# Attention and an expert layer on one core: float64 weights turned in fewer passes, seven-product matmuls for the first two batches too, and the order of every engine as a written list

## The chip, the cores and the metric

One core of a Trainium2 chip runs one program. Its engines are TensorE (PE, with its weight loads PEld), VectorE (DVE), ScalarE (ACT), GpSimd (POOL) and SyncE (SP, which here only issues DMAs). The metric is the device time of one execution in microseconds (us).

## What is computed

For each of 8 batches and 8 heads, 512 tokens of 64 numbers read from 32 state rows by a softmax, and the state rows read from the tokens by another. The results, 544 rows of 512 per batch, go through a normalisation and a two-layer network with a residual:

```python
a = softmax(scale * x @ state.T);   xread = a @ state
a2 = softmax(scale * state @ x.T);  sread = a2 @ x
x = concat([xread, sread])                      # 8 x 544 x 512
xn = (x - mu) / sqrt(var + 1e-06) * g_ln
out = x + max(xn @ w_ch1, 0) @ w_ch2            # 512 -> 2048 -> 512
```

x and state arrive as float32; g_ln as float32; the two weight matrices arrive as float64 and are read as pairs of 32-bit words.

## The kernel before, in words

Every matmul operand is held as a pair of float16 tiles (hi, and lo for what hi leaves out), and a product is three matmuls (`TERMS`). The network's hidden width of 2048 is cut into four units u of 512.

**A batch.** `attention(b)` loads x and the state, scales and splits x, transposes by DMA, makes scores (L214), both softmaxes, `sread` (L259, L269) and the tokens' reads (L300, evicted by ACT on L302). It ends in `normalise`, whose last steps cut the result into pairs `pc` (ACT makes hi, DVE makes lo) and transpose them by DMA into `xnT` (L343). Then come the **first products** (xnT times w_ch1) and the **second products** (hidden times w_ch2, L612), which `ffn` runs for batch b while it pulls `attention(b + 1)` forward a step at a time. After the last batch the sreads of all batches go through the same network as one batch of 256 rows.

**Two kinds of first product.** For batches 2 to 7 and for the state rows, `first_product` forms each 2 x 2 block product from seven half-size products (Strassen's scheme, L570): 336 matmuls of 256 columns per batch, with sums of blocks on DVE and POOL around them. It needs sums of weight blocks (`weight_sums`, made during batch 1) and of xn blocks (`pieces`). For batches 0 and 1 `first_product_plain` (L551) takes 192 matmuls of 512 columns, and `normalise` cuts its pairs without sums (L359).

**The weights.** `convert` turns each unit of either matrix in two halves of 128 x 1024. For a half, ACT takes the sign (L447) and the magnitude (L416) of the high words, DVE bounds it and takes its maximum (L417), shifts it (L418) and joins it with the low words (L419); then, with the unit's scale known, ACT scales (L453), POOL gives the sign back (L454), ACT makes hi (L461) and POOL lo (L462). `common_scale` brings the four units of w_ch2 to one scale when all are there, by multiplying the tiles in place on DVE (L540).

**Order.** The tile framework's scheduler orders each engine's instructions from the order of the code. For the head (batch 0, the attention of batch 1 and all weights) `PLAN` says how many steps of which generator come next; batch 0 goes through the second products unit by unit as weights become ready. Each engine runs its instructions in order, and so does the SP queue with the DMAs.

Of the kernel before, what the change touches and what calls it, by code (L numbers as in the profile page):

```python
# [20 lines left out]
F64_MIN = 2.0**-15  # L21
F64_AMAX = 2.0**-12
# [4 lines left out]
SW1 = 2.0**3  # L27
# [15 lines left out]
TERMS = ((0, 0), (0, 1), (1, 0))  # L43
COMPUTE = (mybir.EngineType.Activation, mybir.EngineType.DVE, mybir.EngineType.Pool)
# [3 lines left out]
def moe_attention(ctx: ExitStack, tc: tile.TileContext, x, state, g_ln, w1, w2, out):  # L48

# [41 lines left out]

    def accumulator():
        return ps_f.tile([P, 512], F32, name="acc")

    def banks():
        return ps_a.tile([P, 2, 512], F32, name="banks")

    def column(pool, name, n=1):
        return pool.tile([P, n], F32, name=name)


    def load_batch(b):
# [12 lines left out]
    loaded = {0: load_batch(0)}
# [20 lines left out]
    def across(a, name):


        n = a.shape[1]
        ps = ps_x.tile([P, 512], F32, name="spread")  # L140
        nc.tensor.transpose(ps[0:n, 0:P], a, idf)
        top = column(small, name + "_t")
        nc.vector.tensor_reduce(top[0:n], ps[0:n, 0:P], AX.X, ALU.max)
        nc.tensor.matmul(ps[:, P:P + n], lhsT=top[0:n].broadcast_to([n, P]), rhs=idf[0:n, 0:n], start=True, stop=True)
        return ps[:, P:P + n]

    def absmax(a, t):
# [15 lines left out]
    marks = {}  # L163
    sread_rows = tc.dram_tile([B * NS, DM], F32, name="sread_rows")

    def attention(b):
        if b not in loaded:
            loaded[b] = load_batch(b)
            yield
        xf, sj, sr = loaded.pop(b)  # L170
        xfl = xf.rearrange("p h c d -> p (h c) d")
        am, part = column(small, "x_am", 2), column(small, "x_part", 4)
        x16 = rows("x16").bitcast(F16).rearrange("p (a i d) -> p a i d", i=2, d=D)
        for q in range(4):
            v = slice(8 * q, 8 * q + 8)
            if q % 2 == 0:
                nc.scalar.activation(x16[:, v].bitcast(BF16)[:, :, 0], xfl[:, v], AF.Abs, accum_out=part[:, q:q + 1])
            else:
                absmax(part[:, q:q + 1], xfl[:, v].rearrange("p a d -> p (a d)"))
            yield  # L180
        absmax(am[:, 0:1], part)
        absmax(am[:, 1:2], sj.rearrange("p g d -> p (g d)"))
        m = column(small, "x_m", 2)
        nc.vector.tensor_scalar_max(m, across(am, "x"), TINY)
        sc, isc = scales(m, SX, "x")
        sx, sst, isx, isst = sc[:, 0:1], sc[:, 1:2], isc[:, 0:1], isc[:, 1:2]
# [547 lines left out]
```

## Time and profile before

| | us |
|---|---|
| median of 3 runs | 864.38 |
| lowest, highest | 862.9, 864.95 |
| the profiled execution, its own time | 863.29 |
| its span, first to last instruction | 861.5 |
| TensorE busy | 742.0 |
| VectorE busy | 543.6 |
| ScalarE busy | 331.3 |
| GpSimd busy | 215.0 |

The profiled execution took 1.8 us more than its span, and 1.1 less than the median. A row of a timeline gives start, duration, engine, line, operation, out<-in and shapes, how many instructions are merged in it, and in brackets the idle time of the engine before it and what ended that. VectorE's instructions overlap a little at their ends, so that one after another they advance by less than their durations.

### The profile page before, as it was taken

The numbers are of one execution on the slowest core, as the hardware profiler recorded it, in microseconds if no ns is written. First come the engines' busy times: TensorE is split into PE (matmuls) and PEld (weight loads), VectorE is DVE, ScalarE is ACT, GpSimd is POOL, SyncE is SP. The second block draws the span as 40 slices with busy tenths as digits, with TensorE's granted clock in tenths as the row PEclk, the third lists the DMA queues.
The fourth block names the chain that finished last, engine by engine and source line by source line (L and its number), as shares of the span: only waits on it lengthen the run. The fifth ranks groups of instructions, "written<-read, shape, count | busy, mean of one in ns | idle before, by whom it ended". The sixth has DMA issues, their size and how long they took to land.

```text
span 861.5 us, 12789 instructions
## 1 busy us (share of the span) xinstructions
PE 742.0 (86%) x5184; PEld 453.2 (53%) x5184; DVE 543.6 (63%) x897; ACT 331.3 (38%) x534; POOL 215.0 (25%) x137
## 2 busy tenths in 40 slices
PE   0230998964999899999989899989998999999997
PEld 0130443521434487548744685478546854784483
DVE  5999778788783568456836584648565856562050
ACT  4484765233541344134413452235234523341030
POOL 0076664175750202021112021202111211020010
PEclk9999999976999999999999999999999999999999
DMA  8952414513033551262333633443335232402000
GB/s 214 314 182 38 159 49 107 138 50 98 10 60 78 121 116 32 53 141 62 60 70 97 112 57 66 118 79 59 76 88 117 51 77 54 107 2 43 25 27 24
DMA packets 146586, 73.83 MB, mean 86 GB/s; under 512 B 125472, under 2 KB 137248, under 8 KB 146080
## 3 DMA queue, kind: packets, MB, share of 16 engines
q1 hardware_dynamic: 146384, 72.77, 35.5%
q8 instruction: 40, 0.66, 0.3%
q10 hardware_dynamic: 144, 0.26, 0.2%
q14 instruction: 18, 0.15, 0.1%
HBM read 28.57 MB, written 9.44 MB: 44 GB/s over the span
## 4 chain that ended last, share of the span: by engine, by line
PE 54%; DVE 20%; DMA 14%; issue 4%; ACT 3%; SPq 3%; POOL 2%; DVEq 0%; ACTq 0%
PE acc L570 24%; PE acc L612 23%; DMA xnT<-pc 5%; PE acc L551 4%; DMA raw<-in_moe_w_ch_dram 3%; DVE pc L383 2%; DVE w_t L419 2%; DMA s_r<-in_state_dram 2%; DVE pc L359 2%; DMA ebT<-eb 2%; DVE x L200 1%; DVE w_t L417 1%; DVE xm L348 1%; DMA x_f<-in_x_dram 1%; SPq L343 1%
## 5 line engine op out<-in xcount | busy, mean ns | idle before, releaser
L612 PE MATMUL acc<-w2h,hid 128*128 128x512 f16 x1632 | 364.4, 382 | 8.5 <-ACT w2h L461 4.1
L570 PE MATMUL acc<-xnT,w1c 128*128 128x256 f16 (+1 forms) x2352 | 250.2, 268 | 14.3 <-DMA xnT<-pc 13.2
L612 PEld LDWEIGHTS <-hid 128*128 128x128 f16 x1632 | 159.2, 99 | 196.3 <-issue 11.7
L570 PEld LDWEIGHTS <-w1c 128*128 128x128 f16 x2352 | 216.6, 99 | 48.1 <-issue 17.6
L551 PE MATMUL acc<-xnT,w1c 128*128 128x512 f16 x384 | 90.4, 391 | 16.8 <-DMA xnT<-pc 16.5
L596 POOL TENSOR_TENSOR m<-u,m 128x512 f32<-128x512 f32 (+1 forms) x28 | 33.4, 1194 | 234.1 <-DVE u L595 174.2
L551 PEld LDWEIGHTS <-w1c 128*128 128x128 f16 x384 | 37.8, 100 | 64.9 <-issue 24.7
L629 DVE SCALAR_TENSOR_TENSOR xr<-acc,uo,xr 128x512 f32<-128x512 f32 x28 | 21.0, 749 | 78.0 <-PE acc L612 78.0
L302 ACT ACTIVATE xr<-banks,ux 128x1024 f32<-128x1024 f32 x14 | 15.6, 1114 | 105.3 <-PE banks L300 103.9
L338 POOL TENSOR_TENSOR rs<-rs,mhalf 128x4 f32<-128x4 f32 (+1 forms) x9 | 12.3, 1367 | 169.7 <-DVE rs L337 120.7
L454 POOL TENSOR_TENSOR w_t<-w_t,sgn 128x1024 f32<-128x1024 f32 x16 | 36.4, 2300 | 62.3 <-ACT w_t L453 62.3
L578 ACT ACTIVATE hid<-u 128x512 f16<-128x512 f32 (+1 forms) x56 | 32.9, 593 | 26.5 <-DVE u L599 21.6
L333 DVE BATCH_NORM_STATS2 s<-xr 128x6 f32<-128x512 f32 x32 | 20.7, 684 | 33.7 <-ACT xr L302 33.7
L579 DVE SCALAR_TENSOR_TENSOR hid<-u,hid 128x512 f16<-128x512 f32 (+1 forms) x56 | 38.9, 707 | 2.1 <-ACT hid L578 2.1
L383 DVE TENSOR_TENSOR pc<-xn,pc 128x512 f16<-128x512 f32 (+1 forms) x28 | 23.7, 878 | 25.0 <-ACT pc L382 25.0
L579 DVE SCALAR_TENSOR_TENSOR hid<-acc,hid 128x512 f16<-128x512 f32 (+1 forms) x28 | 18.1, 645 | 33.3 <-ACT hid L578 33.3
L583 ACT ACTIVATE m<-acc 128x512 f32<-128x512 f32 (+1 forms) x28 | 15.6, 556 | 54.6 <-PE acc L570 40.9
L245 POOL TENSOR_TENSOR ts<-ts,mA 128x1024 f32<-128x1024 f32 x8 | 16.1, 2008 | 54.9 <-DVE mA L244 53.1
L589 ACT ACTIVATE m<-acc 128x512 f32<-128x512 f32 (+1 forms) x28 | 15.8, 566 | 33.7 <-PE acc L570 24.1
L348 DVE SCALAR_TENSOR_TENSOR xm<-xr,mv,gx 128x512 f32<-128x512 f32 x32 | 28.7, 917 | 0.0
L382 ACT ACTIVATE pc<-xn 128x512 f16<-128x512 f32 (+1 forms) x28 | 15.1, 588 | 32.5 <-DMA xnT<-pc 32.4
L554 ACT ACTIVATE hid<-acc 128x512 f16<-128x512 f32 x32 | 18.7, 592 | 22.7 <-PE acc L551 22.7
(128 smaller groups left out, 892.0 us busy)
## 6 DMA issues: line engine op xcount, KB each, us to landing
raw<-in_moe_w_ch_dram SPq DMA_DIRECT2D x16, 1024.0 KB, 6.1
x_f<-in_x_dram SPq DMA_DIRECT2D x16, 512.0 KB, 5.8
out_dram<-xr SPq DMA_DIRECT2D x16, 512.0 KB, 3.0
ek<-ea SPq DMA_DIRECT2D x56, 64.0 KB, 2.0
ek<-ek SPq DMA_DIRECT2D x7, 512.0 KB, 4.2
s_r<-in_state_dram SPq DMA_DIRECT2D x32, 64.0 KB, 5.0
s_j<-in_state_dram SPq DMA_DIRECT2D x8, 64.0 KB, 2.2
sread_rows<-sread SPq DMA_DIRECT2D x32, 16.0 KB, 3.3
```

The lines of the kernel that those rows point to most:

```text
L333: nc.vector.bn_stats(s6, xr[t][:, c])
L348: nc.vector.scalar_tensor_tensor(xm, xr[t][:, c], mv[:, n, 0:1], gx, ALU.subtract, ALU.mult)
L383: nc.vector.tensor_tensor(pc[:, q, 1], v, pc[:, q, 0], ALU.subtract)
L454: nc.gpsimd.tensor_tensor(t, t, sgn[:, fh], ALU.mult)
L551: nc.tensor.matmul(ps, lhsT=w1c[u][:, q // 2 * 2 + k // 2, i, k % 2, q % 2 * P:(q % 2 + 1) * P], rhs=xT[:, k // 2 * 2:k // 2 * 2 + 2, j, k ...
L554: nc.scalar.activation(hid[:, 0, q], ps, AF.Relu)
L570: nc.tensor.matmul(ps[:, f * w:(f + 1) * w], lhsT=w1c[u][:, A_PIECE[m], i, k, f * P:(f + 1) * P], rhs=xT[:, m, j, k * w:(k + 1) * w], star ...
L578: nc.scalar.activation(hi, v, AF.Relu)
L579: nc.vector.scalar_tensor_tensor(lo, v, 0.0, hi, ALU.max, ALU.subtract)
L596: nc.gpsimd.tensor_tensor(m5, u3, m5, ALU.add)
L612: nc.tensor.matmul(po, lhsT=hid[:, i, q, c * P:(c + 1) * P], rhs=w2h[u][:, j, q], start=first and q == 0 and n == 0, stop=last and q == 3 ...
L629: nc.vector.scalar_tensor_tensor(v, po, uo, v, ALU.mult, ALU.add)
```

## The change

**Conversion** (`load`, `split`). Per half, ACT multiplies the high words in place by 2^-112, POOL multiplies them by zero, which leaves a signed zero, DVE joins it with the shifted low words and then with the shifted high words, and ACT takes the sum of magnitudes for the scale. Then ACT makes hi and DVE lo, both with the scale in the instruction. The sums of blocks of w_ch1 are taken by POOL from the float32 values before the split, four per unit, and all seven blocks are split.

**Seven products for all batches.** `first_product_plain`, the plain branch of `normalise` and `weight_sums` are gone. Products are scaled as they leave PSUM, by `hs[u]` and `hn[u]`, so `common_scale` makes four small instructions and no pass over w_ch2. The first of the evicted blocks goes through ACT into a strip `r` before it is split.

**Order.** All functions yield closures, one for each step, and `issue` runs them in the order of the lists `PLAN`, `BATCH` (batches 1 to 6) and `LAST`, with the framework's scheduler off. Of these lists one line is shown.

```diff
-    def magnitudes(raw, t, most):
...
-        nc.scalar.activation(t, raw[:, :, 1].bitcast(F32), AF.Abs)
-        nc.vector.tensor_scalar(t, t, F64_MIN, F64_AMAX, ALU.max, ALU.max, accum_out=most)
-        nc.vector.tensor_scalar(ti, ti, 7 << 27, 3, ALU.bitwise_xor, ALU.logical_shift_left)
-        nc.vector.scalar_tensor_tensor(ti, low, 29, ti, ALU.logical_shift_right, ALU.bitwise_or)
...
-            nc.scalar.activation(t, t, AF.Abs, scale=s)
-            nc.gpsimd.tensor_tensor(t, t, sgn[:, fh], ALU.mult)
...
-            nc.scalar.activation(hi, t, AF.Copy)
-            engine.tensor_tensor(lo, t, hi, ALU.subtract)
...
+            yield do(nc.scalar.activation, high.bitcast(F32), high.bitcast(F32), AF.Copy, scale=REBIAS)
+            yield do(nc.gpsimd.tensor_tensor, t, high.bitcast(F32), zero.broadcast_to([P, 1024]), ALU.mult)
+            yield do(nc.vector.scalar_tensor_tensor, low, low, 29, t.bitcast(U32), ALU.logical_shift_right,
+                     ALU.bitwise_or)
+            yield do(nc.vector.scalar_tensor_tensor, t.bitcast(U32), high.bitcast(U32), 3, low, ALU.logical_shift_left,
+                     ALU.bitwise_or)
+            yield do(nc.scalar.activation, raws[fh].bitcast(BF16)[:, 0:1024], t, AF.Abs, accum_out=am[:, fh:fh + 1])
...
+    def split(hi, lo, t, s):
+        yield do(nc.scalar.activation, hi, t, AF.Copy, scale=s)
+        yield do(nc.vector.scalar_tensor_tensor, lo, t, s, hi, ALU.mult, ALU.subtract)
...
+        yield do(nc.gpsimd.tensor_tensor, s1, a21, a22, ALU.add)
...
-        for u in range(U):
-            v = w2h[u].rearrange("p i q e -> p (i q e)")
-            nc.vector.tensor_scalar(v, v, ratio[:, u:u + 1], None, ALU.mult)
...
+        do(nc.vector.tensor_scalar, hs, uoq, r, SH, ALU.mult, ALU.mult)()
+        nc.vector.tensor_scalar(hn, hs, -1.0, None, ALU.mult)
...
+        yield do(nc.scalar.activation, r, p1, AF.Relu, scale=sp)
+        yield from finish(r, 0, 0)
...
+    "a1 a0 c0 b1 a3 a2 c1 a4-5 b0 a6-12 a60 a13 a27 a19 a28 a17 a20 a14 a18 a24 a15 c2 a16 a25 a22 c3 k2 a23 "
...
+        with tc.manual_schedule():
...
+    issue([attention(0), *map(weights1, range(U)), first_products(0, h, True), *map(weights2, range(U)), attention(1),
+           second_products_by_units()], PLAN)
     common_scale()
...
+    for b in range(1, B - 1):
+        issue([first_products(b, h), second_products(b, h, store_batch), attention(b + 1)], BATCH)
+    issue([first_products(B - 1, h), second_products(B - 1, h, store_batch), state_rows(), first_products(B, 1),
+           second_products(B, 1, store_state)], LAST)
```

**What stands in a row.** Three places on VectorE. In the kernel after, most closures run from one line, so rows read L104 and tell by their tiles: `raw` the float64 words, `w_t` the float32 weights, `w1c` and `w2h` the split weights, `strips` the evicted blocks of a first product, `hid` the split hidden values, `xr` the residual rows, `acc` and `banks` PSUM tiles.

VectorE in the middle of the head, where a half of w_ch2 is turned beside batch 0's first products, before:

```order
L417 TENSOR_SCALAR w_t,w_am<-w_t 128x1024
L555 SCALAR_TENSOR_TENSOR hid<-acc,hid 128x512 x2
L418 TENSOR_SCALAR w_t<-w_t 128x1024
L419 SCALAR_TENSOR_TENSOR w_t<-raw,w_t 128x1024
L555 SCALAR_TENSOR_TENSOR hid<-acc,hid 128x512
L143 TENSOR_REDUCE w_t<-spread 2x1
```

and after:

```order
L104 SCALAR_TENSOR_TENSOR raw<-raw,w_t 128x1024
L104 SCALAR_TENSOR_TENSOR w1c<-sums,w_s,w1c 128x512
L104 SCALAR_TENSOR_TENSOR w_t<-raw 128x1024
L104 SCALAR_TENSOR_TENSOR strips<-acc,strips 128x512
L104 SCALAR_TENSOR_TENSOR w1c<-w_t,w_s,w1c 128x512
```

Between the steps of the conversion there stand now splits of w_ch1, which read two tiles of SBUF each; before there stood evictions, which read PSUM and one tile.

VectorE at the end of the head, where the last scale of w_ch2 is known and batch 1 is normalised, before:

```order
L533 TENSOR_REDUCE uo<-uoq 128x1
L348 SCALAR_TENSOR_TENSOR xm<-xr,mv,gx 128x512 x2
L536 RECIPROCAL r<-uo 128x1
L537 TENSOR_SCALAR ratio<-uoq,r 128x4
L540 TENSOR_SCALAR w2h<-w2h,ratio 128x4096 x3
```

and after:

```order
L104 TENSOR_REDUCE uo<-uoq 128x1
L104 SCALAR_TENSOR_TENSOR xn<-xr,mv,gx 128x2x256
L104 RECIPROCAL r<-uo 128x1
L104 SCALAR_TENSOR_TENSOR w2h<-w_t,w_s,w2h 128x1024
L104 TENSOR_SCALAR hs<-uoq,r 128x4
L104 SCALAR_TENSOR_TENSOR w2h<-w_t,w_s,w2h 128x1024
```

The three passes over a whole unit are gone, and the two lo halves of the last unit stand there, which GpSimd made before.

VectorE around the end of a middle batch, from the second pair of statistics (`rs`) to the last pair of the next batch's `pc`, before:

```order
L337 TENSOR_SCALAR rs<-mv 128x4
L348 SCALAR_TENSOR_TENSOR xm<-xr,mv,gx 128x512
L148 TENSOR_REDUCE x_part<-x_f 128x1
L376 TENSOR_TENSOR tq<-xn 128x512
L383 TENSOR_TENSOR pc<-xn,pc 128x512 x2
L376 TENSOR_TENSOR tq<-xn,tq 128x512
L148 TENSOR_REDUCE x_part<-x_f 128x1
L383 TENSOR_TENSOR pc<-tq,pc 128x512
L629 SCALAR_TENSOR_TENSOR xr<-acc,uo,xr 128x512
```

and after:

```order
L104 TENSOR_SCALAR rs<-mv 128x4
L104 SCALAR_TENSOR_TENSOR xr<-acc,uo,xr 128x512
L104 TENSOR_TENSOR tq<-xn 128x512
L104 TENSOR_TENSOR pc<-xn,pc 128x512
L104 TENSOR_TENSOR tq<-xn,tq 128x512
L104 TENSOR_TENSOR pc<-tq,pc 128x512 x2
L104 TENSOR_TENSOR pc<-xn,pc 128x512 x3
L104 SCALAR_TENSOR_TENSOR xr<-acc,uo,xr 128x512
```

One more eviction of a second product (`xr<-acc`) stands behind the statistics, and the reductions of the following batch's x no longer stand between the pieces.

## Rows read from the trace of the kernel before

**Rows 1.** The page's shares of the chain of work that ended last, by engine.
```profile
PE 54%; DVE 20%; DMA 14%; issue 4%; ACT 3%; SPq 3%; POOL 2%; DVEq 0%; ACTq 0%
```

**Rows 2.** Busy time by stretch: the stretch, its length, then for PE, PEld, DVE, ACT and POOL the busy time (and instructions), then the granted clock of TensorE, the DMA share and GB/s. The cuts are the starts of first products, and in the last three the starts of the last batch's first and second products and of the state rows.
```profile
7.50:85.55 78.05, 15.02 (x168) 11.15 (x168) 72.11 (x126) 47.31 (x62) 32.55 (x14) 1.00 0.66 187
85.55:206.70 121.15, 96.62 (x488) 43.38 (x488) 99.23 (x154) 59.28 (x79) 63.94 (x32) 0.91 0.35 96
...
478.32:563.05 84.73, 84.73 (x619) 55.68 (x619) 53.76 (x89) 33.05 (x58) 13.14 (x9) 0.98 0.42 85
...
652.55:737.48 84.93, 84.93 (x619) 55.72 (x619) 53.43 (x89) 33.33 (x56) 13.17 (x9) 0.98 0.33 72
737.48:775.75 38.27, 37.17 (x338) 32.88 (x337) 24.29 (x41) 14.82 (x27) 7.19 (x7) 1.00 0.17 41
775.75:817.19 41.44, 41.44 (x196) 18.84 (x194) 6.01 (x11) 2.81 (x6) 0.20 (x1) 1.00 0.15 35
817.19:861.50 44.31, 39.48 (x432) 27.91 (x429) 14.13 (x35) 8.48 (x24) 2.92 (x4) 1.00 0.08 25
```

**Rows 3.** Timeline of PE at the starts of batches (and the DMA issue ahead of batch 1's first product): start, us, what.
```profile
202.21 4.30 SPq L343 DMA_TRANSPOSE xnT<-pc  x2
...
206.70 17.18 PE L551 MATMUL acc<-xnT,w1c 128*128 128x512 f16 x72 [13.28 <-DMA xnT<-pc]
...
434.94 1.84 PE L259 MATMUL banks<-ebT,x 128*128 128x64 f16 x32 [2.22 <-DMA ebT<-eb]
...
458.89 15.92 PE L612 MATMUL acc<-w2h,hid 128*128 128x512 f16 x73
478.32 5.76 PE L570 MATMUL acc<-xnT,w1c 128*128 128x256 f16 x36 [3.50 <-DMA xnT<-pc]
...
487.05 13.27 PE L570 MATMUL acc<-xnT,w1c 128*128 128x256 f16 x120
...
569.40 9.34 PE L570 MATMUL acc<-xnT,w1c 128*128 128x256 f16 x84 [2.25 <-DMA xnT<-pc]
...
652.55 5.76 PE L570 MATMUL acc<-xnT,w1c 128*128 128x256 f16 x36 [3.42 <-DMA xnT<-pc]
```

**Rows 4.** Groups of VectorE's instructions from 0 to 206.7 us: line, operation, out<-in, shapes, count | busy us, mean ns | idle before.
```profile
L419 DVE SCALAR_TENSOR_TENSOR w_t<-raw,w_t 128x1024 uint32<-128x1024 uint32 x16 | 26.1, 1633 | 0.1
L417 DVE TENSOR_SCALAR_CACHE_REDUCE w_t<-w_t 128x1024 f32<-128x1024 f32 x16 | 19.4, 1212 | 4.1 <-ACT w_t L416 3.9
L418 DVE TENSOR_SCALAR w_t<-w_t 128x1024 uint32<-128x1024 uint32 x16 | 16.6, 1039 | 0.1
L359 DVE SCALAR_TENSOR_TENSOR pc<-xm,rs,pc 128x256 f16<-128x256 f32 x16 | 15.3, 1011 | 1.8 <-ACT pc L358 1.8
L348 DVE SCALAR_TENSOR_TENSOR xm<-xr,mv,gx 128x512 f32<-128x512 f32 x8 | 11.5, 1445 | 0.0
...
L540 DVE TENSOR_SCALAR w2h<-w2h,ratio 128x4096 f16<-128x4096 f16 x3 | 7.4, 2520 | 0.0
...
L426 DVE TENSOR_SCALAR w_m<-w_m 128x2 uint32<-128x2 uint32 x8 | 3.0, 369 | 0.2
...
L537 DVE TENSOR_SCALAR ratio<-uoq,r 128x4 f32<-128x4 f32 x1 | 1.9, 1900 | 0.0
```

**Rows 5.** Timeline of VectorE and GpSimd in the head: first VectorE's instructions while GpSimd is idle, then VectorE's beside GpSimd's run of four multiplications, then that run.
```profile
26.22 1.22 DVE L419 SCALAR_TENSOR_TENSOR w_t<-raw,w_t 128x1024 uint32<-128x1024 uint32 x1
...
34.91 1.22 DVE L232 SCALAR_TENSOR_TENSOR eb<-eB,eb 128x1024 f16<-128x1024 f32 x1
36.05 0.69 DVE L418 TENSOR_SCALAR w_t<-w_t 128x1024 uint32<-128x1024 uint32 x1
36.65 1.22 DVE L249 TENSOR_REDUCE dA<-ts 128x32 f32<-128x1024 f32 x1
...
190.53 0.73 DVE L348 SCALAR_TENSOR_TENSOR xm<-xr,mv,gx 128x512 f32<-128x512 f32 x1
...
201.71 0.87 DVE L359 SCALAR_TENSOR_TENSOR pc<-xm,rs,pc 128x256 f16<-128x256 f32 x2
...
48.59 2.48 DVE L418 TENSOR_SCALAR w_t<-w_t 128x1024 uint32<-128x1024 uint32 x1
51.11 3.03 DVE L419 SCALAR_TENSOR_TENSOR w_t<-raw,w_t 128x1024 uint32<-128x1024 uint32 x1
...
56.31 1.21 DVE L417 TENSOR_SCALAR_CACHE_REDUCE w_t<-w_t 128x1024 f32<-128x1024 f32 x1
...
48.40 9.81 POOL L454 TENSOR_TENSOR w_t<-w_t,sgn 128x1024 f32<-128x1024 f32 x4 [16.55 <-ACT w_t L453]
```

**Rows 6.** Groups of GpSimd's instructions, over the whole span or (L245) from 0 to 206.7 us: as in Rows 4.
```profile
L454 POOL TENSOR_TENSOR w_t<-w_t,sgn 128x1024 f32<-128x1024 f32 x16 | 36.4, 2300 | 62.3 <-ACT w_t L453 62.3
L245 POOL TENSOR_TENSOR ts<-ts,mA 128x1024 f32<-128x1024 f32 x2 | 3.8, 1914 | 28.2 <-DVE mA L244 28.2
...
L493 POOL TENSOR_TENSOR sums<-sums 128x512 f32<-128x512 f32 x12 | 16.4, 1379 | 0.6
L596 POOL TENSOR_TENSOR m<-u,m 128x512 f32<-128x512 f32 x24 | 30.5, 1271 | 176.4 <-DVE u L595 116.5 <-DVE x_m L184 43.3 <-DVE x_i L132 16.7
```

More of the change, by code (lines that the diff above doesn't have):

```diff
@@ L1 @@
-from contextlib import ExitStack, nullcontext
+from contextlib import ExitStack
 import concourse.bass as bass
@@ L320, in attention, with normalise @@
-            yield
-        yield from normalise(xr, C // 2, b < 2)
+            for j in range(4):
+                px = accumulator().rearrange("p (c g d) -> p c g d", c=C, g=G)
+                yield do(mix, j, px, ea)
+                o = xr_all.rearrange("p c (g j d) -> p c g j d", g=G, j=4)[:, :, :, j]
+                yield do(nc.scalar.activation, o, px, AF.Copy, scale=ux)
+        yield from normalise(xr, C // 2)
     results = []
-    def normalise(xr, cw, plain):
+    def normalise(xr, cw):
@@ new lines, in weights1 @@
+        w1c[u] = w.rearrange("p (m i k f) -> p m i k f", m=7, i=2, k=2)
+        w = w.rearrange("p (m i e) -> p m i e", m=7, i=2)
+        a11, a12, a21, a22 = (t[:, 512 * q:512 * q + 512] for q in range(4))
+        sums = (odd if u % 2 else spare)("sums")
+        s1, s2, s3, s4 = (sums[:, 512 * q:512 * q + 512] for q in range(4))
+        def piece(m, v):
+            return split(w[:, m, 0], w[:, m, 1], v, scale)
+        yield from piece(0, a11)
+        yield do(nc.gpsimd.tensor_tensor, s1, a21, a22, ALU.add)
@@ new lines, in weights2 @@
+        yield from load(src, raws, ts, SW2, "w2", scale, inv)
+        yield do(nc.vector.tensor_scalar, uoq[:, u:u + 1], inv, is1[:, u:u + 1], isg, ALU.mult, ALU.mult)
+        w = wide(u, "w2h").bitcast(F16).rearrange("p (i q e) -> p i q e", i=2, q=4)
+        w2h[u] = w
+        for fh, t in enumerate(ts):
+            q = slice(2 * fh, 2 * fh + 2)
+            yield from split(w[:, 0, q], w[:, 1, q], t.rearrange("p (q e) -> p q e", q=2), scale)
+    uo = main.tile([P, 1], F32, name="uo")
+    hs, hn = main.tile([P, U], F32, name="hs"), main.tile([P, U], F32, name="hn")
@@ L606, in first_product @@
-        hids.append(hid)
-        yield
-    def second_product(po, hid, c, u, first, last):
-        for q in range(4):
-            for n, (i, j) in enumerate(TERMS):
-                nc.tensor.matmul(po, lhsT=hid[:, i, q, c * P:(c + 1) * P], rhs=w2h[u][:, j, q],
-                                 start=first and q == 0 and n == 0, stop=last and q == 3 and n == 2)
-    def ffn(xr, xT, cw, store, work, plain=False):
-        hid = []
-        for u in range(U):
-            for n, _ in enumerate((first_product_plain if plain else first_product)(u, xT, cw, hid)):
-                if plain or (u + n) % 2 == 0:
-                    next(work, None)
-            if plain:
-                weight_sums(u)
+            yield do(nc.scalar.activation, hi, v, AF.Relu)
@@ new lines, in first_product, with multiply @@
+        yield product(4, p2, False)
+        yield add(u3, p2, sp, m1)
+        yield do(nc.gpsimd.tensor_tensor, m5, u3, m5, ALU.add)
+        yield product(5, p3, False)
+        yield add(u2, p3, sp, u2)
+        yield from finish(u2, 0, 1)
+        yield from finish(m5, 1, 1)
+        yield product(6, p4, True)
+        yield add(u3, p4, sn, u3)
+        yield from finish(u3, 1, 0)
+    def second_product(po, hid, c, u, first, last):
+        def multiply(po, hid, w):
+            for q in range(4):
+                for n, (i, j) in enumerate(TERMS):
+                    nc.tensor.matmul(po, lhsT=hid[:, i, q, c * P:(c + 1) * P], rhs=w[:, j, q],
+                                     start=first and q == 0 and n == 0, stop=last and q == 3 and n == 2)
+        return do(multiply, po, hid, w2h[u])
```

679 lines of the change are left out of this document (282 added, 397 removed), and 49 rows, old and new, of tables (BATCH, LAST, PLAN).

## Prediction

> **What bounds the kernel now.** I read the shares of the chain first, then the stretches, then the starts of batches. The chain says PE 54%, DVE 20%, DMA 14% [rows 1]: no single bound, so the stretches must be taken apart [rows 2]. The program has two regimes, and the border is the start of batch 1's first product at 206.70; call it H.
>
> Before H, TensorE is idle for half the time or more: 15.0 busy of 78.1 us, then 96.6 of 121.2. VectorE is busy 72.1 + 99.2 = 171.3 of 199.2 us, ACT 47.3 + 59.3 = 106.6, GpSimd 32.6 + 63.9 = 96.5. So VectorE sets H. Part of that "busy" is waiting: an instruction that finds GpSimd at work is shown long. The join of words L419 takes 1.22 us while GpSimd is idle and 3.03 beside its run of four multiplications; the shift L418 0.69 and 2.48; the bound with accumulation L417, with one input, stays at 1.21 in that same run [rows 5].
>
> After H, TensorE is the bound. Two middle batches take 84.73 and 84.93 us with PE busy throughout [rows 2]. Yet at each batch's start PE had stood still, for 3.50, 2.25 and 3.42 us, waiting for the DMA that transposes the normalised tokens, and at 434.94 for 2.22 more; after the first of these, 36 matmuls take 5.76 us (0.160 each) where 120 warm ones take 13.27 (0.1106): 1.8 us lost again [rows 3]. The 73 second-product matmuls that stand as cover before such a start last 15.9 us (0.218 each); the chain behind them lasts 478.32 - 458.89 = 19.4.
>
> **H: VectorE's own work.** What waiting is in the 171.3? For each group, count times (mean - duration undisturbed): L419 16 x (1.63 - 1.22) = 6.6; L418 16 x (1.04 - 0.69) = 5.6; L359 16 x (1.01 - 0.43) = 9.3 (two of them take 0.87); L348 8 x (1.45 - 0.73) = 5.7; L426 8 x (0.37 - 0.16) = 1.7; L537 1.7 [rows 4, 5] (0.16 for a row of two or four numbers is my estimate). With some 2 us in small groups: 32. Work without waits: 171.3 - 32 = 139. One behind another, VectorE advances by 1.14 us per instruction of 1024 elements and by 0.60 at 512 (34.91, 36.05, 36.65 in [rows 5]); I use these steps.
>
> Removed: of the conversion 19.4 (L417) + 16 x 0.60 (L418) + 16 x 1.14 (L419) = 47.2; the passes of L540, 7.4 [rows 4]; batch 0's 16 plain evictions, 16 x 0.60 = 9.6; batch 1's 16 half-width pieces, 16 x 0.35 = 5.6; block sums, maxima and updates that go to GpSimd or behind H, 13 x 0.60 = 7.6. Sum 77.4.
>
> Added: two joins for each of 16 halves, 32 x 1.14 = 36.5; 28 splits of w_ch1 blocks at 0.61 = 17.1; 8 lo halves of w_ch2 at 1.14 = 9.1; batch 0's seven-product evictions, 30 x 0.60 = 18; 15 more piece and difference steps of batch 1 at 0.60 = 9.0. Sum 89.7. VectorE's work becomes 139 - 77.4 + 89.7 = **151**, more than before: the passes saved in the conversion pay for work that moves in from GpSimd.
>
> **H: the waits.** GpSimd in the head falls from 96.5 to about 73: 16 multiplications by zero x 2.0 = 32 (L245 takes 1.91, L454 2.30), 16 block sums x 1.3 = 21 (L493 1.38, L596 1.27), and some 20 for attention, normalise and strips at the same rates [rows 6]. Before, waits were 32 of 96.5, a third of GpSimd's busy time. But then only some 62 of VectorE's 139 us were instructions that wait as L419 and L418 do: 18 of L419, 10 of L418, 6 each of L359 and L348, and by my count of attention's steps 22; L417 and the PSUM evictions were free of it. After, it is 62 - 18 - 10 - 6 + 36.5 + 17.1 + 9.1 + 9.0 and some 5 of batch 0's evictions that read strips: 104 of 151. The share goes from 0.45 to 0.69. VectorE also has fewer idle gaps for GpSimd to work in (5% below, not 14%: 0.95 / 0.86 = 1.1). So I scale: 33% x (0.69 / 0.45) x 1.1 = 56% of 73 = **41**. The bounds are 24 (a third, as before) and 73 (all of it).
>
> Idle time of VectorE before H was 199.2 - 171.3 = 28; with the order written out and all blocks ready ahead I take 9, bounds 5 and 28. Start at 7.5; from the last pieces to the first matmul 4.5 (202.21 to 206.70, [rows 3]). H = 7.5 + 151 + 41 + 9 + 4.5 = **213**, 6 us later than now. ACT does not take over: it drops one pass per half and is at half load. TensorE neither: batch 0's first product will start later, since w_ch1's seven blocks must be split first, but after it only some 83 us of matmuls stand before H (first and second products of a batch, 37 + 41, and batch 1's attention).
>
> **After H.** A middle batch without its cold start is 84.8 - 1.8 = 83.0 us of PE. Batch 1 becomes one of them: H to 478.32 now lasts 271.6 for batches 1 to 3, that is 90.5 each. Six batches, 1 to 6: 498. The last batch's products 38.27 + 41.44 - 1.1 (37.17 busy in the first) = 78.6; state rows 39.5; the idle in their stretch 44.31 - 39.48 = 4.8 stays, for no step there changes [rows 2]. Sum 620.9.
>
> The stalls now cost some 20.6 us over batches 2 to 7 (the four of [rows 3], smaller ones like them, and the cold starts). The new lists put 108 second-product matmuls, 108 x 0.218 = 23.3 us, between the last use of PE by `attention` and the next batch's start, where 73 gave 15.9; the chain to be covered lasts 19.4. It loses the two reductions of x that stood between the pieces, and gains one eviction. So the cover suffices by some 4 us, and I leave 3 us of stalls in all, and 2 for a cold start at H. What is late next is PE itself. Span 213 + 620.9 + 2 + 3 = 838.9; the profiled execution lies 1.8 above its span: 840.7, say **841**. That execution is 1.1 below the median, which I leave in the range. Against 863.3 this is 22.6 less, nearly all from behind H; the head gives nothing.
>
> **Rivals.**
> R1, slower: GpSimd and VectorE take turns over the head. If each microsecond of GpSimd holds VectorE up for one, W = 73 instead of 41: +32, 873. It decides from W = 65 (41 + 23.7). For it: L419 at 3.03 is 1.22 + 1.81, nearly one multiplication, and the new stream puts joins and splits, all with two inputs in SBUF, back to back. Against it: in the mean the waits were a third, and some instructions (PSUM evictions, reductions) remain beside which GpSimd runs. Chance 0.13. The Trainium skill ("SBUF — State Buffer", section "Who interferes with whom") states the rule of this rival: a VectorE instruction with two SBUF inputs contends with a GpSimd instruction that reads SBUF, and the port pair is held for a whole instruction. By that rule the time comes out at 873 if no evictions or idle gaps take GpSimd in; the trace agrees in its single rows (3.03 and 2.48), and not in the sums, where two thirds of GpSimd's time went by without a wait.
> R2: the stalls at batch starts stay as they are, because some other link (statistics on GpSimd, ACT's pieces, the queue of transposes behind other DMAs) is late: 20.6 instead of 5, +16, 857. For it: a written order can't adapt, and one eviction more stands ahead of the pieces. Against: 23.3 us of cover for 19.4. Chance 0.16.
> R3, slower: the joins read every second word of the pairs, and so cost double: +32 x 1.14 = 36, 877. Against: L419 read the low words in this way at 1.22, as long as a contiguous row of that size [rows 5]. Only the second join, the high words in a two-input form, is new. Chance 0.05.
> R4: the order gives GpSimd its turns beside evictions, so that W = 24 and idle 5: -21, 820. Chance 0.12.
> That the lists change little and the head merely loses what the batches gain, ending within 0.2% of 864.4 (862.7 to 866.1, about what a measurement of this kernel can tell from no change): 0.06.
>
> **How the numbers follow.** Forecast 841, chance 0.48; R4 0.12, R2 0.16, no change 0.06, R1 0.13, R3 0.05. Faster: 0.48 + 0.12 + 0.16 = 0.76; same 0.06; slower 0.18. The range goes from just below R4 (818, W at its lower bound) to R1 (873); it leaves out R3, half of R1 above 873 and the part of R4 below 818, about 0.15.
>
> **What would show it.** H at about 213 with VectorE busy over 90% of the head and GpSimd near 73 bears out the head; H near 195 is R4, near 245 R1. The joins' rows tell R3 from R1: a shortest instance near 1.2 us with a long mean is waiting, a shortest near 2.3 is R3. At the starts of batches 2 to 7, waits for the transposes of `pc` under 1 us and a period of 83 us bear out the second half; waits of 3 us are R2. I am wrong if the period falls below 82, since no matmul of a middle batch is removed, or if PE, not VectorE, holds H.

## The result, and the profile after

The median is 871.76 us (870.05 to 872.99) against 863.9 before, four executions each: ratio 1.0089, interval 1.0066 to 1.0113, 0.9% slower where 2.6% faster was forecast. The profiled execution has a span of 870.8. In the kernel after, H, the start of batch 1's first product, is at 232.34.

The chain's shares and the stretches, with the columns of [rows 1] and [rows 2]; the first stretch is the whole head, the next four are parts of it, then four of the six middle batches and the last batch's first products:

```profile
PE 54%; DVE 21%; DMA 9%; ACT 7%; SPq 5%; issue 3%; POOL 1%; DVEq 0%; ACTq 0%; POOLq 0%
...
7.50:232.34 224.84, 114.63 (x798) 72.73 (x799) 195.13 (x282) 115.44 (x180) 86.52 (x45) 0.91 0.46 123
...
99.82:145.62 45.80, 27.74 (x165) 19.99 (x165) 41.36 (x64) 30.22 (x51) 14.67 (x7) 0.72 0.27 72
145.62:232.34 86.72, 71.68 (x467) 41.38 (x466) 68.62 (x103) 34.03 (x52) 19.56 (x11) 0.91 0.37 89
99.82:232.34 132.52, 99.42 (x631) 61.37 (x631) 109.98 (x167) 64.24 (x102) 34.24 (x17) 0.85 0.34 83
160.35:232.34 71.99, 65.50 (x442) 39.01 (x443) 57.46 (x92) 32.35 (x50) 15.75 (x9) 0.93 0.33 81
...
232.34:318.24 85.90, 83.25 (x621) 54.92 (x619) 55.15 (x89) 38.19 (x64) 14.45 (x9) 1.00 0.43 92
318.24:406.47 88.23, 84.79 (x620) 55.46 (x619) 54.19 (x87) 37.60 (x63) 14.45 (x9) 0.98 0.38 81
406.47:491.13 84.66, 83.11 (x620) 55.05 (x619) 54.21 (x87) 37.60 (x63) 14.46 (x9) 1.00 0.39 85
491.13:575.18 84.05, 83.01 (x620) 55.04 (x619) 54.20 (x87) 37.59 (x63) 14.46 (x9) 1.00 0.39 84
...
743.58:783.52 39.94, 37.35 (x326) 32.50 (x325) 24.61 (x39) 17.68 (x30) 6.85 (x6) 0.96 0.12 34
```

Against [rows 2], the head is 25.6 us longer (232.34 - 206.70), the six middle batches 19.5 shorter (511.2 for 530.8), and what follows 3.2 longer (127.2 for 124.0): +9.3, the difference of the spans. So the gain behind the head came, and the head took it and more.

VectorE in the head, groups with the columns of [rows 4], and below them the largest group of GpSimd:

```profile
L104 DVE SCALAR_TENSOR_TENSOR raw<-raw,w_t 128x1024 uint32<-128x1024 uint32 x16 | 26.6, 1664 | 1.7 <-POOL w_t L104 1.7
L104 DVE SCALAR_TENSOR_TENSOR w_t<-raw 128x1024 uint32<-128x1024 uint32 x16 | 25.2, 1582 | 0.2
L104 DVE SCALAR_TENSOR_TENSOR w1c<-sums,w_s,w1c 128x512 f16<-128x512 f32 x16 | 14.7, 935 | 0.0
L104 DVE SCALAR_TENSOR_TENSOR hid<-strips,hid 128x512 f16<-128x512 f32 x16 | 14.4, 909 | 0.0
L104 DVE SCALAR_TENSOR_TENSOR w1c<-w_t,w_s,w1c 128x512 f16<-128x512 f32 x12 | 12.9, 1091 | 0.0
...
L104 POOL TENSOR_TENSOR w_t<-raw,zero 128x1024 f32<-128x1024 f32 x16 | 37.7, 2374 | 34.4 <-DMA raw<-in_moe_w_ch_dram 15.3 <-DVE w1c L104 10.6 <-ACT raw L104 5.0
```

Four single joins, the first two beside GpSimd, the others while it is idle; they say what a join costs alone:

```profile
19.37 2.92 DVE L104 SCALAR_TENSOR_TENSOR raw<-raw,w_t 128x1024 uint32<-128x1024 uint32 x1
22.33 2.80 DVE L104 SCALAR_TENSOR_TENSOR w_t<-raw 128x1024 uint32<-128x1024 uint32 x1
25.05 1.21 DVE L104 SCALAR_TENSOR_TENSOR raw<-raw,w_t 128x1024 uint32<-128x1024 uint32 x1
26.36 1.22 DVE L104 SCALAR_TENSOR_TENSOR w_t<-raw 128x1024 uint32<-128x1024 uint32 x1
```

Count times (mean - duration alone) over all groups of the head gives an estimate of 41 us of waits (7.3 and 6.0 for the two joins, 3.3, 3.7 and 4.2 for the next three rows, the rest in small groups). VectorE's own work is then 195.1 - 41 = 154, and its idle time 224.84 - 195.13 = 29.7, where [rows 2] has 27.9.

VectorE's longest wait stands in the middle of the head. VectorE, then the DMA queue, ACT and TensorE:

```profile
146.55 4.03 DVE L104 SCALAR_TENSOR_TENSOR hid<-strips,hid 128x512 f16<-128x512 f32 x3
150.51 0.74 DVE L104 SCALAR_TENSOR_TENSOR x<-x_f,x_s,x 128x512 f16<-128x512 f32 x1
...
166.00 1.22 DVE L104 TENSOR_REDUCE mB<-banks 128x2 f32<-128x1024 f32 x1 [8.89 <-PE banks L300]
...
151.32 1.32 SPq L104 DMA_TRANSPOSE xT<-x  x1
152.70 1.31 SPq L522 DMA_DIRECT2D raw<-in_moe_w_ch_dram  x1
154.06 1.21 SPq L104 DMA_TRANSPOSE sT<-sh  x1
155.31 4.64 SPq L104 DMA_TRANSPOSE xT<-x  x1
...
159.63 1.12 ACT L104 ACTIVATE raw<-raw 128x1024 f32<-128x1024 f32 x1 [12.34 <-DMA raw<-in_moe_w_ch_dram]
...
160.35 1.05 PE L300 MATMUL banks<-xT,sT 128*32 128x512 f16 x8 [7.98 <-DMA sT<-sh]
```

The last of four splits of batch 1's x stands on VectorE behind three splits of hidden values; the first transposition of x starts when it ends (by the program, the transposed x takes the buffer that this split still reads); behind that in the SP queue wait a load of w_ch2, on which ACT stands 12.3 us, and the state's transposition, on which TensorE stands 8.0; VectorE then waits 8.9 for the scores.

### The profile page after: what moved, and what is told of

The parts are those of the page before. It is cut to its first block, busy times and chain, and to the rows that moved or that the text cites. A ratio compares the mean times of both kernels' runs of the same rounds, so it can differ in the third digit from the quotient of the medians.

```text
span 870.8 us, 13433 instructions
## 1 busy us (share of the span) xinstructions
PE 734.7 (84%) x5472; PEld 483.9 (56%) x5472; DVE 571.0 (66%) x895; ACT 376.2 (43%) x624; POOL 185.7 (21%) x117
## 4 chain that ended last, share of the span: by engine, by line
PE 54%; DVE 21%; DMA 9%; ACT 7%; SPq 5%; issue 3%; POOL 1%; DVEq 0%; ACTq 0%; POOLq 0%
PE acc L608 28%; PE acc L568 22%; SPq L104 5%; DVE strips L104 4%; DVE hid L104 3%; DMA ek<-ek 3%; DMA sT<-sh 2%; DVE w_t L104 2%; DVE w1c L104 2%; DVE raw L104 2%; DMA ek<-ea 2%; ACT x L104 2%; ACT raw L104 1%; ACT hid L104 1%; DVE x L104 1%
## 5 line engine op out<-in xcount | busy, mean ns | idle before, releaser
L568 PE MATMUL acc<-xnT,w1c 128*128 128x256 f16 (+1 forms) x3024 | 331.6, 272 | 21.1 <-DMA xnT<-pc 7.7
L568 PEld LDWEIGHTS <-w1c 128*128 128x128 f16 x3024 | 285.6, 100 | 63.7 <-issue 22.3
L104 ACT ACTIVATE hid<-strips 128x512 f16<-128x512 f32 (+1 forms) x144 | 85.5, 604 | 127.6 <-DVE strips L104 88.8
L104 POOL TENSOR_TENSOR strips<-strips 128x512 f32<-128x512 f32 (+1 forms) x36 | 50.8, 1419 | 306.6 <-DVE strips L104 248.5
L104 DVE SCALAR_TENSOR_TENSOR hid<-strips,hid 128x512 f16<-128x512 f32 (+1 forms) x144 | 105.5, 753 | 15.7 <-ACT hid L104 14.7
L104 ACT ACTIVATE strips<-acc,hs 128x512 f32<-128x512 f32 (+1 forms) x96 | 61.7, 657 | 97.2 <-PE acc L568 95.4
L104 DVE SCALAR_TENSOR_TENSOR strips<-acc,hs,strips 128x512 f32<-128x512 f32 (+1 forms) x96 | 66.5, 705 | 52.9 <-PE acc L568 48.8
L104 DVE SCALAR_TENSOR_TENSOR xr<-acc,uo,xr 128x512 f32<-128x512 f32 x28 | 21.0, 749 | 75.3 <-PE acc L608 75.3
L104 ACT ACTIVATE xr<-banks,ux 128x1024 f32<-128x1024 f32 x14 | 15.6, 1115 | 75.0 <-PE banks L382 75.0
L104 DVE TENSOR_TENSOR pc<-xn,pc 128x512 f16<-128x512 f32 (+1 forms) x36 | 31.6, 900 | 24.5 <-ACT pc L104 24.5
L104 POOL TENSOR_TENSOR rs<-rs,mhalf 128x4 f32<-128x4 f32 (+1 forms) x9 | 10.4, 1154 | 169.3 <-DVE rs L104 169.2
L104 POOL TENSOR_TENSOR w_t<-raw,zero 128x1024 f32<-128x1024 f32 x16 | 37.7, 2374 | 34.4 <-DMA raw<-in_moe_w_ch_dram 15.3
L104 DVE SCALAR_TENSOR_TENSOR strips<-acc,hn,strips 128x512 f32<-128x512 f32 (+1 forms) x32 | 22.6, 705 | 23.2 <-PE acc L568 23.2
L104 ACT ACTIVATE xn<-xn,rs 128x512 f32<-128x512 f32 x34 | 22.1, 712 | 35.7 <-POOL rs L104 35.7
L104 ACT ACTIVATE pc<-xn 128x512 f16<-128x512 f32 (+1 forms) x36 | 20.7, 599 | 33.9 <-DMA xnT<-pc 33.5
L104 DVE BATCH_NORM_STATS2 s<-xr 128x6 f32<-128x512 f32 x32 | 20.7, 685 | 20.6 <-ACT xr L104 20.6
L104 POOL TENSOR_TENSOR ts<-ts,mA 128x1024 f32<-128x1024 f32 x8 | 17.2, 2148 | 75.0 <-DVE mA L104 75.0
L104 PE MATMUL spread<-idf,w_am 128*2 128x128 f32 x8 | 2.9, 359 | 31.4 <-ACT raw L104 29.3
L104 ACT ACTIVATE raw<-w_t 128x1024 bf16<-128x1024 f32 x16 | 16.8, 1052 | 27.2 <-DVE w_t L104 25.8
```

What stands on the lines that cost most here:

```text
L104: return lambda: f(*map(now, args), **{k: now(v) for k, v in kw.items()})
L568: nc.tensor.matmul(ps[:, f * w:(f + 1) * w], lhsT=w1u[:, m, i, k, f * P:(f + 1) * P], rhs=xTk[:, m, j, k], start=begin and f == 0 and k == ...
```

## The experiments

Theory A: the head ends late because the written order leaves engines idle. Theory B: it ends late because VectorE's instructions wait while GpSimd works. Medians stand beside the 871.76 of the changed kernel; ratios are to the kernel before on the same chip. The kernel before had medians of 861.8 to 863.9 there, so two medians of different chips tell nothing below some 2 us, and the end of a head is that of one profiled execution.

**e1 and e2: the written order taken away,** in the head, or behind it.

```diff
-        with tc.manual_schedule():
+        with (ExitStack() if plan is PLAN else tc.manual_schedule()):
...
-        with tc.manual_schedule():
+        with (tc.manual_schedule() if plan is PLAN else ExitStack()):
```

> The changed kernel with the framework's scheduler on in the head (the list gives only the order of the code), the lists of the later batches as written. Theory A: the head ends late (232.3 us) because the written order leaves engines idle: VectorE 29.7 us and TensorE 33 us after its first product, evictions and splits of x queued behind conversion steps. Then the scheduler, which takes what is ready, ends the head 10 to 25 us earlier: total 847 to 862. Theory B: the head is long because VectorE waits for the port shared with GpSimd (39 us) and has more work; then the order matters little: 866 to 877.

875.88 us (1.0163, interval 1.0142 to 1.0184), outside what A said and inside B's range. The head:

```profile
7.50:233.63 226.13, 106.64 (x798) 69.72 (x799) 194.75 (x283) 115.07 (x179) 89.72 (x45) 0.97 0.46 123
```

VectorE is busy for the same 194.75 us and as idle (31.4). The first products begin at 127.94 and TensorE then runs with 14 us of idle. So the written order, as a whole, is no loss against the scheduler's.

> The changed kernel with the written order in the head alone; the later batches go through the framework's scheduler. If the gain behind the head (six batches in 511 us where before took 531) comes from the written order, it is lost: 880 to 892, with waits of 2 to 4 us for the transposes of pc at the starts of batches again. If it comes only from the seven products of batch 1 (4 us) and from passes saved, the time stays within 4 us of 871.8.

877.85 us (1.0195, 1.0170 to 1.0220): 6 us lost, between the two ranges. The six batches take 515.9 in place of 511.2:

```profile
232.44:748.35 515.91, 499.49 (x3716) 330.55 (x3714) 328.05 (x522) 225.99 (x378) 88.98 (x54) 1.00 0.38 81
```

Waits for `pc` are back only as 0.5 to 0.7 us at the starts of two batches. Most of the 19.5 us thus does not come from the written order. TensorE's time says more: over the six batches it is busy 512.3 us before, 499.5 here and 500.3 in the changed kernel, and idle 18.5, 16.4 and 10.9. So 12 of the 19.5 us are shorter busy time, which comes with the scheduler too, and the written order takes idle time away. By batch, 9.8 of the 19.5 fall to batch 1 (95.66 to 85.90), which lost its plain products; since the scheduler here still reads the code in the lists' sequence, the rest is not separated further.

**e3: the zero from ACT.** It leaves out the signs of the weights, as do e6 and e7.

```diff
-            yield do(nc.gpsimd.tensor_tensor, t, high.bitcast(F32), zero.broadcast_to([P, 1024]), ALU.mult)
+            yield do(nc.scalar.activation, t, high.bitcast(F32), AF.Copy, scale=0.0)
```

> The changed kernel with the multiplication by zero on ACT in place of GpSimd (16 passes of 1024, 37.7 us of GpSimd's 86.5 in the head go, ACT gets 16 x 1.1 = 18 us). Theory B: VectorE's waits fall from 39 us to about 22 and the head ends 12 to 17 us earlier: 855 to 860. Theory A: VectorE's waits fall likewise, but TensorE's late start and the list set the end: at most 6 us earlier, 866 to 872, and VectorE's idle time in the head grows by what its waits lose.

854.68 us (0.9916, 0.9889 to 0.9943). The head, as a stretch:

```profile
7.50:214.99 207.49, 110.85 (x799) 70.53 (x800) 174.17 (x282) 131.03 (x195) 48.20 (x29) 0.96 0.49 134
```

GpSimd is busy 38.3 us less, VectorE 21.0 less for the same instructions, and the head ends 17.4 earlier. That is B, a little beyond its ranges; VectorE's idle time grew by 3.6 only.

**e4: one move in the list.** The last quarter of batch 1's x is split right behind the third.

```diff
-h18 k30-31 h20 i7 h19 g22 h21 k32 h23 f34 k33 h22 g23 k21 h24 f28 k26 f36 f35 ... l14 k27 j7 l7 k28 i4
+h18 k30-31 k26 h20 i7 h19 g22 h21 k32 k27 h23 f34 k33 k28 h22 g23 k21 h24 f28 f36 f35 ... l14 j7 l7 i4
```

> The changed kernel with one move in the head's list: the last quarter of batch 1's x is split right behind the third, not behind three pairs of hidden values, and its transposes are issued with the others. Theory A: the scores start some 8 us earlier (152 in place of 160.4), TensorE's wait of 8.0 us for sT shrinks, and as TensorE is busy from there on, the head ends 5 to 8 us earlier: 864 to 867. Theory B: no change, 870 to 873.

862.38 us (0.9999, 0.9984 to 1.0014), level with the kernel before. The head as a stretch, the DMA queue, and TensorE's first scores:

```profile
7.50:222.28 214.78, 111.64 (x799) 71.94 (x799) 195.16 (x282) 115.61 (x179) 86.63 (x45) 0.93 0.48 129
...
140.34 4.93 SPq L104 DMA_TRANSPOSE xT<-x  x2
145.36 0.53 SPq L522 DMA_DIRECT2D raw<-in_moe_w_ch_dram  x1
145.99 1.71 SPq L104 DMA_TRANSPOSE sT<-sh  x1
...
152.91 0.62 PE L300 MATMUL banks<-xT,sT 128*32 128x512 f16 x8
```

VectorE's busy time is the same to 0.03 us, its idle time falls from 29.7 to 19.6, and the head ends 10.1 earlier, more than the 5 to 8 expected. This is A, narrowed to one place of the list.

**e5 and e10: the conversion in the kernel before,** first the change's own, then that of e8. The shared steps are left out.

```diff
-            nc.scalar.activation(sgn[:, fh], v[:, :, 1].bitcast(F32), AF.Sign)
-            magnitudes(v, ts[fh], am[:, fh:fh + 1])
+            nc.scalar.activation(high.bitcast(F32), high.bitcast(F32), AF.Copy, scale=2.0 ** -112)
+            nc.gpsimd.tensor_tensor(t, high.bitcast(F32), zero.broadcast_to([P, 1024]), ALU.mult)
+            nc.vector.scalar_tensor_tensor(low, low, 29, t.bitcast(U32), ALU.logical_shift_right, ALU.bitwise_or)
...
+            nc.scalar.activation(hi, t, AF.Copy, scale=s)
+            nc.vector.scalar_tensor_tensor(lo, t, s, hi, ALU.mult, ALU.subtract)
```

> The kernel before with the new conversion alone (GpSimd's signed zero, two joins on VectorE, ACT's sum of magnitudes, scale in hi and lo, all lo halves on VectorE); the plain products, the pass over w_ch2 and the scheduler stay. VectorE's own work: -47.2 of the old steps, +32 x 1.14 of joins and +16 x 1.14 of lo halves = +7.5 us; GpSimd loses L454 (36.4) and both groups of L462 (39.6) and gains 16 multiplications by zero (37.7): 58 in place of 96.5, so at 0.45 to 0.55 of wait for each us its part of the waits falls from 32 to some 26 to 30. If so, the conversion is about neutral: 858 to 870 beside 863.9. If the conversion itself is what makes the changed kernel slower, 872 or more.

869.99 us (1.0075, 1.0049 to 1.0102), at the upper end of "about neutral". The head ends at 206.94, where it did before (206.70):

```profile
7.50:206.94 199.44, 107.29 (x655) 53.51 (x655) 167.39 (x274) 92.62 (x142) 63.92 (x32) 0.95 0.50 137
```

The profiled run loses 4.4 us behind it, 3.6 of them idle time of TensorE; why was not followed up.

> e5 (the kernel before with the new conversion) with the conversion of e8 in place of GpSimd's signed zero and the first join. If GpSimd's multiplications are what the conversion costs, VectorE loses some 21 us of waits (0.55 x 37.7) and 8 us of work against e5: 840 to 852, below the kernel before too. If the scheduler's order or TensorE bounds that head, 860 to 868.

843.93 us (0.9780, 0.9750 to 0.9810). With GpSimd out of the conversion:

```profile
7.50:182.35 174.85, 106.78 (x655) 53.41 (x655) 147.87 (x274) 93.31 (x142) 28.60 (x16) 0.96 0.58 156
```

The head of the kernel before ends 24.4 us earlier, and some 5 us are lost behind it, as in e5. Against e5, VectorE is busy 19.5 us less: 8.5 are work (16 x (1.21 - 0.68), a shift in place of a join) and 11.0 waits, for 35.3 us of GpSimd less. B holds there too, but at 0.31 us of wait for each us of GpSimd and not at the 0.55 of the expectation; the rest of the gain is 5 us less idle time of VectorE.

**e6 and e7: both causes removed, and two moves more.** `zero` holds minus zero here.

```diff
+            yield do(nc.scalar.activation, t, high.bitcast(F32), AF.Identity, bias=zero, scale=0.0)
...
-i7 h19 ... h24 f28 f36 f35 k22 j1 f30 g24 ... k75 j12 f71 j13 f66 j14 f73 j15
+i7 f28 f30 h19 ... h24 f36 f35 k22 j1 g24 ... k75 f71 j12 f66 j13 f73 j14 j15
```

> The changed kernel with the x move of e4 and the zero on ACT, now as an identity with scale 0 and a bias of minus zero. If VectorE's waits (e3: 17 us) and the late quarter of x (e4: 9 us) are separate causes, the gains add up: head's end at 205 to 208, total 843 to 848. If both only remove the same idle time of TensorE, the total stays at 852 to 857.

848.27 us (0.9823, 0.9781 to 0.9864), head's end 210.15. Of e3's 17.1 and e4's 9.4 us, 23.5 came together, and of the heads' 17.4 and 10.1 it is 22.2: two causes that add up for the most part.

> e6 with two more moves in the head's list: ACT's two evictions of batch 0 ahead of three hi halves of w_ch2 (TensorE waited 5.7 us for them in e4), and TensorE's small transposition for the last unit's maximum behind a product that was ready (4.3 us of wait in e4). If TensorE bounds the head's second half, 3 to 8 us less than e6: 836 to 844; if VectorE does, within 2 us of e6.

850.00 us (0.9860, 0.9801 to 0.9920): no gain, and within the 2 us that the expectation gives to VectorE. TensorE's wait for ACT's evictions fell from 5.7 to 2.2 us, but waits of 1.5 and 0.6 for the next inputs followed, and the wait for the copies of `ek` grew from 1.1 to 3.4. There TensorE follows a chain of steps; taking one wait off its queue moves the wait.

**e8, e9, e11, e12: the sign from ACT as an exponent bit, then the sums on VectorE, then the scheduler again.**

```diff
-            yield do(nc.scalar.activation, high.bitcast(F32), high.bitcast(F32), AF.Copy, scale=REBIAS)
-            yield do(nc.gpsimd.tensor_tensor, t, high.bitcast(F32), zero.broadcast_to([P, 1024]), ALU.mult)
-            yield do(nc.vector.scalar_tensor_tensor, low, low, 29, t.bitcast(U32), ALU.logical_shift_right,
-                     ALU.bitwise_or)
+            yield do(nc.scalar.activation, high.bitcast(F32), high.bitcast(F32), AF.Prelu, scale=REBIAS, alpha=-2.0 ** 32)
+            yield do(nc.vector.tensor_scalar, low, low, 29, None, ALU.logical_shift_right)
...
-        yield do(nc.gpsimd.tensor_tensor, s1, a21, a22, ALU.add)
+        yield do(nc.vector.tensor_tensor, s1, a21, a22, ALU.add)
```

> The changed kernel with the x move of e4 and a conversion without GpSimd that gives the right sign: ACT scales the high words by 2^-112 with a slope of -2^32 for negative ones, so that the sign stands as one exponent bit which the shift by 3 brings to the top; VectorE shifts the low words in place (one input) and joins once. GpSimd loses 37.7 us as in e6, and 16 of VectorE's 32 joins have one input in place of two. If the waits for the shared port are what costs, VectorE's busy time in the head falls from 195 to 165 to 174 and the total is 836 to 848 (e6: 848.3). If a pass of ACT in GpSimd's place is what helped e3 and e6, this has the same number of ACT's passes as the changed kernel and stays at 855 to 862.

838.28 us (0.9721, 0.9694 to 0.9748). It has as many passes of ACT as the changed kernel and GpSimd's load of e6: it is GpSimd's absence that counts, and not a pass of ACT. Against e4 VectorE is busy 28.9 us less, 8.5 of them work as in e10 and 20.4 waits for 39.2 us of GpSimd: 0.52.

> e8 with the 16 block sums of w_ch1 on VectorE in place of GpSimd (26.5 us of GpSimd go, VectorE gets 16 x 0.60 = 9.6). e3 gave 21 us of VectorE's busy time for 38.3 us of GpSimd's, 0.55 each. At that rate 14.6 us of waits go for 9.6 of work: 3 to 7 us less than e8. If waits count for less here, or the sums lengthen VectorE's chain to the first product, 0 to 6 us more than e8.

835.14 us (0.9687, 0.9659 to 0.9715), 3.1 less than e8.

> e9 with the remaining sums and differences of blocks on VectorE too (in the head four strips and four differences of 1.6 us each go from GpSimd, in each later batch six of 1.3 us). At 0.55 of wait for each us of GpSimd: 7 us less of waits for 8 x 0.60 = 4.8 of work in the head, and nothing behind it, where TensorE is the bound: 0 to 3 us less than e9. If VectorE's evictions come late for TensorE in the later batches, 2 to 8 us more.

832.69 us (0.9649, 0.9625 to 0.9673), the fastest of all. The heads of e8, e9 and e11, and e8's shift of the low words:

```profile
7.50:202.22 194.72, 112.86 (x798) 72.09 (x799) 166.25 (x283) 116.19 (x180) 47.47 (x29) 0.95 0.54 145
...
7.50:197.30 189.80, 112.20 (x799) 71.91 (x799) 163.96 (x299) 115.46 (x180) 22.38 (x13) 0.95 0.54 148
...
7.50:194.31 186.81, 108.16 (x798) 70.21 (x799) 163.37 (x306) 115.50 (x180) 9.02 (x5) 0.95 0.55 149
...
L104 DVE TENSOR_SCALAR raw<-raw 128x1024 uint32<-128x1024 uint32 x16 | 10.9, 682 | 0.0
```

From e8 to e9 GpSimd loses 25.1 us and VectorE's busy time falls by 2.3 although it does 16 x 0.60 = 9.6 more: 11.9 us of waits, 0.47 per us of GpSimd. From e9 to e11 it is 0.6 + 4.8 = 5.4 for 13.4: 0.40. In e3 it was 0.55, from e4 to e8 0.52, and from e5 to e10, in the kernel before, 0.31.

> e11 with the framework's scheduler on in the head, as e1 was for the changed kernel. In e1 the scheduler began batch 0's first products at 127.9 in place of 99.8 and then kept TensorE nearly without waits; the head ended 1.3 us later. If the written list, made for other durations, is what leaves VectorE idle 23 us in e11's head, the scheduler ends it 3 to 10 us earlier: 822 to 830. If the late start of the first products costs again, 833 to 842.

843.20 us (0.9772, 0.9732 to 0.9811), a little above the second range: the scheduler starts the first products at 103.20 (e11: 81.85) and ends the head at 201.03 (194.31). The written list of the head is worth 10 us here, 6.7 of them before H.

## Why the prediction was wrong, step by step

- **VectorE's work and waits in the head: right, the waits by luck in part.** Forecast 151 and 41, measured 154 and 41 (by the estimate above). In the 41 two misses cancel: GpSimd was busy 86.5, not 73, since its own instructions take longer beside VectorE (2.37 us each for the multiplications, 1.89 the shortest, 2.0 forecast), and a microsecond of it cost 0.47, not 0.56. The scaling itself was sound: "a third" in the kernel before is 0.31 from e5 to e10, and the changed kernel's 0.40 to 0.55 is more, as forecast. R1's price of one for one did not come, though the total landed, by other causes, beside its 873. The Trainium skill ("SBUF — State Buffer", section "Who interferes with whom") says that the port pair is held for a whole instruction: single joins agree (2.92 beside GpSimd, 1.21 alone), while the rate over a head, measured by taking GpSimd's work away, was 0.31 to 0.55. Of the two rows that the prediction counts for the rule, 2.48 is that of a shift with one input, which the rule as it quotes it does not cover.
- **VectorE's idle time: the step that failed.** "With the order written out and all blocks ready ahead I take 9", with 4.5 for the last transposition: 13.5. Measured 29.7, so 16 of the 31.9 us by which the span missed (870.8 against 838.9). No row of the trace carried the 9. A written order says what comes next, not that it is ready: one quarter of x in the wrong place cost 10.1 us of idle and 9.4 of the total (e4). Under the scheduler the idle time is 31.4 (e1), so the list is not its only cause. What the other 19.6 us are due to was not separated; of the 29.7, 14.5 stand behind 160.35, where TensorE is the busier engine.
- **"TensorE neither": failed with it.** Forecast 83 us of matmuls behind the start of batch 0's products. Measured 99.4 busy and 33.1 idle from 99.82 to H, at a mean granted clock of 0.72 and then 0.91, between the two levels of 1.2 and 2.4 GHz. Twelve matmuls early and late in that stretch:

```profile
113.65 2.72 PE L568 MATMUL acc<-xnT,w1c 128*128 128x256 f16 x12 [4.23 <-DVE strips L104]
...
190.30 1.47 PE L568 MATMUL acc<-xnT,w1c 128*128 128x256 f16 x12
```

  The forecast took the price of the second row and a queue without waits. From 160.35 on TensorE is busy 65.5 of 72.0 us, so what delays its scores delays H: in e4 the scores start 7.4 us earlier and H comes 10.1 earlier. And H itself is held by TensorE:

```profile
223.70 8.81 PE L608 MATMUL acc<-w2h,hid 128*128 128x512 f16 x40 [2.17 <-DVE hid L104]
232.34 8.18 PE L568 MATMUL acc<-xnT,w1c 128*128 128x256 f16 x72
```

  Batch 1's first product follows 40 second-product matmuls of batch 0 without a wait, where TensorE stood 13.28 us for the transposed `pc` before [rows 3]; the last thing that those 40 waited for, 2.17 us long, was a split of VectorE's. That is the sign of being wrong that the prediction named: PE, not VectorE, holds H. VectorE's sum does not run up to H, and part of its idle time is what TensorE's queue leaves over.
- **Middle batches: the mechanism right, the stalls too small.** TensorE is busy 83.0 to 83.3 us per batch in three of the four shown, as forecast, and the waits for the transposed `pc` are gone: R2 is out. But 498 + 2 + 3 = 503 became 511.2. In their place stand waits for the copies of `ek` (softmax weights that DMAs spread out for the tokens' reads; 0.6 to 2.1 us per batch, 6.7 in all), for the transposed state `sT` (2.0 in all), and for the maximum of x, which is 0.36 each time; and one wait for `ek` was followed by slow matmuls:

```profile
377.67 0.91 PE L382 MATMUL banks<-sk,ek 128*128 128x64 f16 x16 [2.12 <-DMA ek<-ek]
378.42 4.44 PE L608 MATMUL acc<-w2h,hid 128*128 128x512 f16 x12
```

  Twelve matmuls of that line take 2.75 elsewhere; the granted clock was 0.98 over that batch and 1.00 over the other three shown. "What is late next is PE itself" was wrong by 1.4 us a batch.
- **The end.** 127.2 for 122.9: 2.4 of it is a wait for VectorE's strips in the last batch's first product, at 753.94. The 60 matmuls behind it take 8.4 us where 0.1106 each [rows 3] makes 6.6, and another wait takes 0.2.
- **R3 is out**: joins alone take 1.21 and 1.22. **R4** did not come by the list, but its head (H near 195) is what e9 and e11 reach (197.3 and 194.3) with GpSimd out of the way and the quarter of x moved.
- The sum of the misses: head 19.3 (232.3 for 213), batches 8.2, end 4.3: 31.9.

So the head grew by 25.6 us, 23.8 of them VectorE's busy time (195.1 for 171.3), which the conversion's savings did not pay for, and 16.3 came back behind it. The conversion is not what lengthened the head, for with it alone H stays (e5). e1 and e5 share the new conversion and the scheduler in the head, and H is 233.63 in e1 for 206.94 in e5, VectorE busy 194.75 for 167.39, GpSimd 89.72 for 63.92. They differ in the seven products of the first two batches, with their splits and sums, and in the order of the code that the scheduler reads; no run parts these two. The forecast counted the work of the seven products, so it can be why the head is longer, and is not why the forecast missed. Two causes in the head were taken out by themselves: GpSimd's multiplications, 17 us (e3), which are as long as its signs L454 were before (37.7 and 36.4 us), and one late step in a list of several hundred, 9 us (e4); without both it is 848 (e6).

## What to carry to other kernels

Idle time is a term like any other: when a change writes an order by hand, take the idle time of the trace before (28 us here) until a row says why it should fall, and look in the new order for a step whose successors stand behind it in other queues. Work given to GpSimd is not free for VectorE: it cost 0.31 us of VectorE's time for each us of GpSimd in the kernel before and 0.40 to 0.55 in the changed one, where by the prediction's count more of VectorE's instructions read two tiles of SBUF. There 1.66 us of a sum on GpSimd was dearer than 0.60 on VectorE (e9). When two engines both look unbound, sum the second one's work too, at the clock that it will have there, and ask which of them will hold the border.

## What the runs showed of the hardware

VectorE's busy time in a head with the same instructions was 195.1, 194.8 and 195.2 us under three orders (changed kernel, e1, e4), of which the first and the last differ in one place: the waits for GpSimd were the same in all three. VectorE's shift of every second word in place took 0.68 us at 1024 elements, about half of a join's 1.21: 16 x 0.53 = 8.5 of the 8.9 us of VectorE's busy time by which e8 is below e6. A slope for negative inputs on ACT cost as much as a plain scaling:

```profile
L104 ACT ACTIVATE raw<-raw 128x1024 f32<-128x1024 f32 x16 | 18.1, 1132 | 6.9 <-DMA raw<-in_moe_w_ch_dram 6.9
```

The same row of the changed kernel has a mean of 1123 ns.
